# Attention and feed-forward on one core: the range check read from sums that other steps already make

## The chip, the cores and the metric

The kernel runs on one core of a Trainium2 chip. The metric is the device time of the whole launch in microseconds (us), and the lower the better. The core has a matrix engine (PE, whose weight loads the profile lists as PEld), VectorE (DVE), ScalarE (ACT), GpSimd (POOL) and SyncE (SP), which here only starts transfers. Each engine works through its own instructions strictly in order.

## The reference

Attention of four batches, eight heads, 768 tokens, 64 columns a head; a token sees itself and the 95 before it, and the first eight tokens of its batch. Its output, 3072 rows of 512, goes through a feed-forward layer with 2048 hidden columns.

```python
scores = scale * np.matmul(q, k.transpose(0, 1, 3, 2)) + bias          # bias: -slope * distance
scores = np.where(keep, scores, -1000000000.0)
a = np.exp(scores - max); a = a / (sum(a) + 1e-09)
x = np.matmul(a, v)                                                    # then heads side by side: 3072 x 512
h = x @ w_in                                                           # 512 -> 2048
g = np.where(h >= 1, h, np.where(h <= -1, 0.0, (h + 1) ** 2 / 4.0))
out = g @ w_out                                                        # 2048 -> 512
```

All data is f32. The kernel keeps that accuracy with f16 matmuls: a number is split into a high half (its f16 rounding) and a low half (what is left), and three products of halves stand for one product.

## The kernel before, in words

**Tiling.** 24 units of 128 tokens (four batches of six) go through attention. Two units make a chunk of 256 tokens; 12 chunks go through the feed-forward layer, each in eight groups of 256 hidden columns. A unit fetches q, k and v blocks (L754), splits them (high half on ACT, L760; low half on POOL or DVE, L767 to L776), computes scores on PE (L821), adds bias and finds maxima (DVE, L640), takes exponentials with their sums (ACT, L652), splits (L835, L837), turns the result by a transposing transfer on SP's queue (L844), multiplies by v on PE (L862), scales by the reciprocal sums to `x` (DVE, L702), splits that (`xh`: ACT L876, DVE L878), and turns it by another transposing transfer (`xt`, L886).

**Feed-forward.** `ffn1` (L947) makes the 24 matmuls of a group, `h`, in PSUM. `gelu` works on it in steps: s0 on ACT (L970, `u` = relu of h plus a constant, which comes from the one-column tile `half`; the same instruction sums its result into a column of `su`), s1 and s2 on DVE (L980: max; L982: min and product). Steps s3 on split the result into `ga` and `gb`: additions and the low halves on POOL (L992 to L996, L1001, L1006), the high halves on ACT (L999, L1004). From chunk 3 on the second product is made from sums and differences of blocks (L1060, folded into the output `ob` at L1111); the first three chunks use plain products (L1016, with `ob` written at L1133). Hence `u_g` of chunk 10, group g, passes ACT, DVE, POOL, ACT, POOL before PE can use it.

**Weights.** During the first 100 us the weights are split as well: `w_bits` and `wd` on DVE (L535, L539, L543), `woh` and `wd` on ACT (L556, L563), `wol` on POOL (L575).

**The range check.** The fast path holds only for inputs in a certain range. Tests write statistics into columns of the tile `stat`: minima, sums, squares `sq`, the sums `su`. ACT squares each fetched block of q, k and v in place and sums the squares into a column of `sq` (`conv_check`, L784). `verdict` (L1147) compares all of it with limits on DVE, step 0 in ten small instructions (L1150, nine on L1163 and L1164), and where a limit is passed a second, general program runs (`general_path`).

**Order.** Every step is entered in a list `plan` with `at(time, function, ...)`. The written table `PLACE` (L107) then says in which order the plan's steps are issued:

```python
with tc.manual_schedule():
    for n in PLACE or range(len(plan)):
        t, _, f, args = plan[n]
        f(*args)
```

A second written table, `SLOTS`, names the buffer of every tile. Semaphores are placed by the framework from what each instruction reads and writes.

Of the kernel before, what the change touches and what calls it, by code (L numbers as in the profile page):

```python
# [9 lines left out]
F16 = mybir.dt.float16  # L10
F32 = mybir.dt.float32
I32 = mybir.dt.int32
AF = mybir.ActivationFunctionType
# [4 lines left out]
P = 128  # L18
# [14 lines left out]
SV = 256.0  # L33
SW = 4096.0
# [7 lines left out]
NQKV = 3 * NU - B  # L42
W_MAX = NQKV
# [42 lines left out]
CHK = 5.61  # L86
# [203 lines left out]
TPO = 0  # L290
EARLY = 5
R4 = 9
GM = "d"
WL = "pppppppppppppppppppppppppppppppp"
LATE = 8.11
SB = [-25.236754012213545, -6.90594381646442]
# [1206 lines left out]
```

## Time and profile before

| | us |
|---|---|
| runs | 592.34, 591.11, 590.81 |
| median | 591.11 |
| profiled execution, its span | 589.9 |
| PE busy in it | 573.4 (97%) |
| DVE, ACT, POOL busy | 466.4, 442.7, 499.2 |

The profile's span runs from the first to the last instruction. The launch's own time is measured from outside and has some time around the span; for the profiled execution only the span is known, and it is 1.2 us below the median of the runs. A busy share is the part of the span in which an engine had an instruction at work. In a list of instructions the brackets at a row's end say how long the engine stood idle before it and what ended that. The granted clock, PEclk, is 1.00 where TensorE runs at 2.4 GHz and 0.50 where it runs at 1.2 GHz.

### The profile page before, as it was taken

How to read it: one execution, taken by the hardware profiler on the slowest of the kernel's cores; microseconds unless marked ns; L12 is line 12 of the kernel's file. 1: busy time of each engine (PE TensorE's matmuls, PEld its weight loads, DVE VectorE, ACT ScalarE, POOL GpSimd, SP SyncE). 2: the span in 40 equal slices, each digit the busy share in tenths (PEclk: the TensorE clock that was granted, in tenths of full speed). 3: DMA queues.
4: the chain of work that ended last, by engine and by line, in shares of the span. 5: the costliest groups of instructions: out<-in, count | busy, mean ns of one | idle time of the engine just before them, and what ended most of it. 6: DMA issues, size and time to landing. Idle time of an engine off the chain costs nothing.

```text
span 589.9 us, 16477 instructions
## 1 busy us (share of the span) xinstructions
PE 573.4 (97%) x6243; PEld 476.1 (81%) x6243; DVE 466.4 (79%) x1151; ACT 442.7 (75%) x1154; POOL 499.2 (85%) x570
## 2 busy tenths in 40 slices
PE   7999999998999999999999999999999999999995
PEld 5777765456777688987888888889888889898884
DVE  7999999987986767686887977878979877884321
ACT  6999999987956988776986887868868768635340
POOL 0799999977899999899899998799799799579771
PEclk9999999998999999999999999999999999999999
DMA  8796764896650654959856768777688767350011
GB/s 265 235 301 214 236 215 143 184 161 136 131 125 11 144 114 90 192 139 194 211 148 141 133 185 177 179 188 185 153 157 163 184 160 164 87 123 2 1 37 42
DMA packets 145003, 89.24 MB, mean 151 GB/s; under 512 B 108436, under 2 KB 125076, under 8 KB 144916
## 3 DMA queue, kind: packets, MB, share of 16 engines
q1 hardware_dynamic: 144912, 88.10, 60.7%
q8 instruction: 51, 0.84, 0.6%
q14 instruction: 36, 0.29, 0.2%
q10 hardware_dynamic: 4, 0.00, 0.0%
HBM read 54.53 MB, written 6.29 MB: 103 GB/s over the span
## 4 chain that ended last, share of the span: by engine, by line
PE 77%; DVE 9%; ACT 6%; DMA 5%; issue 2%; SPq 0%; DVEq 0%; ACTq 0%
PE h L947 36%; PE o L1060 27%; PE o L1016 5%; PE s L821 4%; PE av L862 4%; DMA pt<-ph 2%; DVE wd L543 2%; ACT z L652 1%; DMA xt<-xh 1%; DVE u L982 1%; DVE w_bits L539 1%; DVE h L980 1%; DMA wd<-in_moe_w_in_dram 1%; DVE w_bits L535 1%; ACT wd L563 1%
## 5 line engine op out<-in xcount | busy, mean ns | idle before, releaser
L947 PE MATMUL h<-xt,wih 128*128 128x256 f16 x1536 | 257.5, 274 | 2.8 <-DMA xt<-xh 2.0
L947 PE MATMUL h<-xt,wil 128*128 128x256 f16 x768 | 210.2, 274 | 0.0
L947 PEld LDWEIGHTS <-wih 128*128 128x128 f16 x1536 | 148.9, 98 | 27.0 <-DVE u L982 3.8
L980 DVE SCALAR_TENSOR_TENSOR h<-h,u 128x512 f32<-128x512 f32 x96 | 66.4, 693 | 37.8 <-ACT u L970 37.5
L1001 POOL TENSOR_TENSOR ga<-u,ga 128x512 f16<-128x512 f32 x72 | 86.9, 1209 | 10.3 <-ACT ga L999 10.1
L652 ACT ACTIVATE z<-z,stat 128x256 f32<-128x256 f32 (+1 forms) x192 | 91.5, 479 | 3.5 <-DVE stat L640 3.1
L1060 PEld LDWEIGHTS <-ga 128*128 128x128 f16 x864 | 83.1, 98 | 10.1
L970 ACT ACTIVATE u<-h,half 128x512 f32<-128x512 f32 x96 | 65.2, 679 | 31.3 <-PE h L947 20.8
L947 PEld LDWEIGHTS <-wil 128*128 128x128 f16 x768 | 75.3, 98 | 9.1
L992 POOL TENSOR_TENSOR u<-u 128x256 f32<-128x256 f32 x72 | 61.5, 856 | 21.0 <-DVE u L982 19.8
L1006 POOL TENSOR_TENSOR gb<-u,gb 128x384 f16<-128x384 f32 x72 | 71.1, 990 | 5.8 <-ACT gb L1004 5.7
L1060 PE MATMUL o<-wd,ga 128*128 128x256 f16 x432 | 70.8, 273 | 0.0
L1060 PE MATMUL o<-woh,ga 128*128 128x256 f16 x288 | 70.7, 273 | 0.0
L999 ACT ACTIVATE ga<-u 128x512 f16<-128x512 f32 x72 | 44.4, 622 | 34.9 <-POOL u L994 26.7
L1060 PEld LDWEIGHTS <-gb 128*128 128x128 f16 x648 | 62.3, 98 | 8.1 <-issue 0.6
L982 DVE SCALAR_TENSOR_TENSOR u<-u,h 128x512 f32<-128x512 f32 x96 | 65.2, 680 | 3.4 <-issue 0.2
L837 DVE SCALAR_TENSOR_TENSOR ph<-z,ph 128x1024 f16<-128x1024 f32 x40 | 54.8, 1373 | 13.3 <-ACT ph L835 13.2
L640 DVE CUSTOM_DVE_ANT_0 z<-s,bias 128x256 f32<-128x256 f32 x160 | 58.9, 414 | 5.8 <-PE s L821 5.7
L1016 PE MATMUL o<-woh,ga 128*128 128x512 f16 x192 | 61.8, 380 | 0.9 <-ACT ob L1133 0.9
L1060 PE MATMUL o<-wd,gb 128*128 128x256 f16 x432 | 60.4, 273 | 0.6 <-DVE ob L1111 0.6
L607 DVE TENSOR_REDUCE stat<-c_raw 128x1 f32<-128x256 f32 x128 | 48.7, 407 | 8.2 <-DMA c_raw<-in_moe_w_in_dram 5.2
L1016 PEld LDWEIGHTS <-ga 128*128 128x128 f16 x288 | 27.2, 98 | 30.2 <-issue 1.9
(131 smaller groups left out, 1166.3 us busy)
## 6 DMA issues: line engine op xcount, KB each, us to landing
wd<-in_moe_w_in_dram SPq DMA_DIRECT2D x16, 512.0 KB, 4.7
wd<-in_moe_w_out_dram SPq DMA_DIRECT2D x16, 512.0 KB, 4.2
c_raw<-in_moe_w_in_dram SPq DMA_DIRECT2D x32, 256.0 KB, 3.2
c_raw<-in_moe_w_out_dram SPq DMA_DIRECT2D x32, 256.0 KB, 3.2
kr<-in_k_dram SPq DMA_DIRECT2D x28, 256.0 KB, 3.8
vr<-in_v_dram SPq DMA_DIRECT2D x28, 256.0 KB, 3.7
qr<-in_q_dram SPq DMA_DIRECT2D x24, 256.0 KB, 4.1
out_dram<-ob SPq DMA_DIRECT2D x23, 256.0 KB, 3.3
```

What stands on the lines that cost most here:

```text
L640: nc.vector.tensor_tensor_reduce(out=p32[u, hf][:, hh, :], in0=pts[u, hf][hh // 2][:, hh % 2, 0:n], in1=(own_bias if n == P else bias)[:, ...
L652: nc.scalar.activation(z, z, AF.Exp, bias=nm[:, c : c + 1], scale=-1.0, accum_out=sums[:, c : c + 1])
L837: nc.vector.scalar_tensor_tensor(phs[u, hf][:, 1, :], zf, SP_, phs[u, hf][:, 0, :], op0=ALU.mult, op1=ALU.subtract)
L947: nc.tensor.matmul(hp[:, :, e, :], w[:, dc, f], xt[:, hf, 2 * a + j, :], start=(n == 0), stop=(n == 3 * NDC - 1),)
L970: nc.scalar.activation(u, h, AF.Relu, bias=half, scale=2.0 / (SV * SW), accum_out=su[:, col : col + 1])
L980: nc.vector.scalar_tensor_tensor(h, h, 4.0 / (SV * SW), u, op0=ALU.mult, op1=ALU.max)
L982: nc.vector.scalar_tensor_tensor(u, u, 4.0, h, op0=ALU.min, op1=ALU.mult)
L992: nc.gpsimd.tensor_sub(f[:, 3:7:3], f[:, 0:6:5], f[:, 4:5].to_broadcast([P, 2, P]))
L1001: nc.gpsimd.tensor_sub(gas[c, g][:, 1], f[:, 0:4], gas[c, g][:, 0])
L1006: nc.gpsimd.tensor_sub(gbs[c, g][:, 1, 0:3], f[:, 4:7], gbs[c, g][:, 0, 0:3])
L1016: nc.tensor.matmul(po, a, w[:, f, :], start=(f == 0 and n == 0), stop=(f == NFC - 1 and n == 2))
L1060: nc.tensor.matmul(acc[:, e], x, w, start=first and n == 0, stop=last and n == 2)
```

## The change

- The 68 instructions of `conv_check` are gone (24 blocks of k, 24 of v, 20 of q), and their 68 columns of `stat`.
- In their place the scaling to `x` (L702 before, L699 after) sums its result into a column of `sq`, for the 40 half units behind the first four units.
- `gelu`'s step s0 takes its constant as a number and sums nothing; the sum `su` is now made by step s2 on DVE.
- A new step `overflow` of four tiny instructions (one on ACT, one on POOL, two on DVE, the last of which writes three columns) tests what the engines make of a conversion that overflows f16.
- `x` is scaled by 128 in place of 256; the limits in `verdict` change.
- `PLACE` is numbered anew for the shorter plan.

```diff
 def scale_x(u, hf):
+    col = 2 * (u - B) + hf
     nc.vector.scalar_tensor_tensor(
-        x, avs[u, hf], SV if u < B else 1.0 / SP_, rs[u, hf].unsqueeze(2).to_broadcast([P, 4, D]),
-        op0=ALU.mult, op1=ALU.mult,
+        x, avs[u, hf], XV if u < B else XV / (SV * SP_), rs[u, hf].unsqueeze(2).to_broadcast([P, 4, D]),
+        op0=ALU.mult, op1=ALU.mult, accum_out=sq[:, col : col + 1] if u >= B else None,
     )
-def conv_check(u, kind, j):
-    b, i = UNITS[u]
-    after(("lo", kind, b, j))
-    r = fetched[u, kind, j]
-    col = {"v": 0, "k": NU, "q": 2 * NU - B}[kind] + (u if kind == "q" else b * NB + j)
-    scale = 1.0 if he(kind, u) != "v" else SV if kind == "v" else SQK
-    nc.scalar.activation(r, r, AF.Square, scale=scale, accum_out=sq[:, col : col + 1])
...
 def gelu(c, g, s):
     if s == 0:
-        col = c * (NFC // 2) + g
-        nc.scalar.activation(
-            u, h, AF.Relu, bias=half, scale=2.0 / (SV * SW), accum_out=su[:, col : col + 1]
-        )
+        nc.scalar.activation(u, h, AF.Relu, bias=2.0, scale=2.0 / (XV * SW))
     elif s == 1:
-        nc.vector.scalar_tensor_tensor(h, h, 4.0 / (SV * SW), u, op0=ALU.mult, op1=ALU.max)
+        nc.vector.scalar_tensor_tensor(h, h, 4.0 / (XV * SW), u, op0=ALU.mult, op1=ALU.max)
     elif s == 2:
-        nc.vector.scalar_tensor_tensor(u, u, 4.0, h, op0=ALU.min, op1=ALU.mult)
+        col = c * (NFC // 2) + g
+        nc.vector.scalar_tensor_tensor(
+            u, u, 4.0, h, op0=ALU.min, op1=ALU.mult, accum_out=su[:, col : col + 1]
+        )
...
+def overflow(s):
+    if s == 0:
+        nc.scalar.activation(c16[:, 0:1], probe[:, 0:1], AF.Copy, scale=SQK)
+    elif s == 1:
+        nc.gpsimd.tensor_add(c16[:, 1:2], probe[:, 0:1], probe[:, 1:2])
+    elif s == 2:
+        nc.vector.scalar_tensor_tensor(
+            c16[:, 2:3], probe[:, 0:1], -SV, probe[:, 1:2], op0=ALU.mult, op1=ALU.subtract
+        )
+    else:
+        nc.vector.tensor_single_scalar(cint, c16.bitcast(I16), 0x7FFF, op=ALU.bitwise_and)
+        nc.vector.tensor_single_scalar(rest[:, 3:6], cint, float(0x7C00), op=ALU.is_equal)
...
 def verdict(s):
-            (sq[:, 0:W_MAX], sq[:, 0:W_MAX], ALU.is_le, 3.6e9),
+            (sq[:, 0:W_MAX], sq[:, 0:W_MAX], ALU.is_le, 1.0e30),
-        nc.vector.tensor_reduce(rest[:, 3:4], stat[:, 0 : marks[4] + 3], axis=AX.X, op=ALU.min)
+        nc.vector.tensor_reduce(rest[:, 6:7], stat[:, 0 : marks[4] + 6], axis=AX.X, op=ALU.min)
-        nc.vector.tensor_single_scalar(su, su, 4000.0, op=ALU.is_le)
+        nc.vector.tensor_single_scalar(su, su, 60000.0, op=ALU.is_le)
```

On PE, SP and POOL the instructions stand in the same order as before, but for one tiny addition on POOL. On ACT the squares are missing. On DVE the three tiny instructions of `overflow` are new, and one block stands elsewhere. Three places of the order follow; a row there gives the line, the operation, what it writes and reads, and the size.

The first is DVE near the end of the attention work. In the kernel before, the block of `verdict` (L1150 to L1164) stands directly ahead of the last unit's two `x` (L702). `h_5`, `h_6` and their `u` belong to groups 5 and 6 of chunk 10.

```order
L1150 TENSOR_REDUCE stat<-stat 128x16
L1163 TENSOR_SCALAR stat<-stat 128x192 x2
L1163 TENSOR_SCALAR stat<-stat 128x68
L1163 TENSOR_SCALAR stat<-stat 128x64
L1163 TENSOR_SCALAR stat<-stat 128x16
L1163 TENSOR_SCALAR stat<-stat 128x64
L1163 TENSOR_SCALAR stat<-nval 128x1 x3
L1164 TENSOR_REDUCE stat<-stat 128x1
L702 SCALAR_TENSOR_TENSOR x_0_9289<-av_0_9250,r_0_9096 128x256
L878 TENSOR_TENSOR xh_0_9292<-x_0_9289,xh_0_9292 128x256
L702 SCALAR_TENSOR_TENSOR x_1_9349<-av_1_9309,r_1_9154 128x256
L980 SCALAR_TENSOR_TENSOR h_5_9214<-h_5_9214,u_5_9335 128x512
```

In the changed kernel DVE's rows just behind the same `x_1` read (L955 and L958 are the gelu's two DVE steps, L867 the low half of `xh`, L1144 to L1158 the block):

```order
L955 SCALAR_TENSOR_TENSOR h_5_9142<-h_5_9142,u_5_9263 128x512
L867 TENSOR_TENSOR xh_1_9281<-x_1_9277,xh_1_9281 128x256
L958 SCALAR_TENSOR_TENSOR u_5_9263,stat<-u_5_9263,h_5_9142 128x2x256
L1144 TENSOR_REDUCE stat<-stat 128x16
L1157 TENSOR_SCALAR stat<-stat 128x192 x2
L1157 TENSOR_SCALAR stat<-stat 128x40
L1157 TENSOR_SCALAR stat<-stat 128x64
L1157 TENSOR_SCALAR stat<-stat 128x16
L1157 TENSOR_SCALAR stat<-stat 128x64
L1157 TENSOR_SCALAR stat<-nval 128x1 x3
L1158 TENSOR_REDUCE stat<-stat 128x1
L955 SCALAR_TENSOR_TENSOR h_6_9104<-h_6_9104,u_6_9296 128x512
```

The whole block has moved behind the last unit's two `x`, whose sums it now reads, and behind the gelu of group 5; it stands directly ahead of the gelu of group 6.

The second place is ACT around 95 to 101 us, where the last weights are split. Before, with `qh_3` the high half of a block of q, `z` exponentials and `woh` weights:

```order
L988 ACTIVATE ga_7_1479<-u_7_1357 128x512
L784 ACTIVATE vr_2_1007,stat<-vr_2_1007 128x512
L760 ACTIVATE qh_3_1492<-qr_3_1354 128x512
L652 ACTIVATE z_0_1484,stat<-z_0_1484,stat 128x256 x4
L652 ACTIVATE z_1_1499,stat<-z_1_1499,stat 128x256
L835 ACTIVATE ph_0_1526<-z_0_1484 128x1024
L556 ACTIVATE woh<-wd 128x512
L563 ACTIVATE wd<-wd 128x512
```

After:

```order
L966 ACTIVATE ga_7_1474<-u_7_1354 128x512
L757 ACTIVATE qh_3_1486<-qr_3_1351 128x512
L648 ACTIVATE z_0_1479,stat<-z_0_1479,stat 128x256 x4
L648 ACTIVATE z_1_1493,stat<-z_1_1493,stat 128x256
L824 ACTIVATE ph_0_1520<-z_0_1479 128x1024
L552 ACTIVATE woh<-wd 128x512
L559 ACTIVATE wd<-wd 128x512
```

The square of a block of v is gone and nothing else has moved; it is the same at the other 67 squares.

The third place is ACT at 123 to 129 us, ahead of the turning of `xh_1`. Before:

```order
L760 ACTIVATE vh_3_1968<-vr_3_1856 128x512
L876 ACTIVATE xh_0_2023<-x_0_1961 128x256
L1048 ACTIVATE wd<-df_1852 128x1024
L784 ACTIVATE qr_5_1615,stat<-qr_5_1615 128x512
L784 ACTIVATE vr_3_1856,stat<-vr_3_1856 128x512
L652 ACTIVATE z_1_2035,stat<-z_1_2035,stat 128x256
L876 ACTIVATE xh_1_2051<-x_1_1956 128x256
```

After:

```order
L757 ACTIVATE vh_3_1959<-vr_3_1848 128x512
L865 ACTIVATE xh_0_2014<-x_0_1952 128x256
L1026 ACTIVATE wd<-df_1844 128x1024
L648 ACTIVATE z_1_2025,stat<-z_1_2025,stat 128x256
L865 ACTIVATE xh_1_2040<-x_1_1947 128x256
```

Two squares that stood ahead of `xh_1` are gone.

## Rows read from the trace of the kernel before

**Rows 1.** The page's list of busy time, share of the span and instructions.

```profile
PE 573.4 (97%) x6243; PEld 476.1 (81%) x6243; DVE 466.4 (79%) x1151; ACT 442.7 (75%) x1154; POOL 499.2 (85%) x570
```

**Rows 2.** Stretches: us, PE, PEld, DVE, ACT, POOL busy, PEclk, DMA share, GB/s.

```profile
80.00:100.00 20.00, 20.00 (x148) 10.74 (x146) 19.83 (x44) 19.96 (x50) 19.54 (x18) 1.00 0.63 197
...
120.00:140.00 20.00, 17.73 (x220) 11.14 (x220) 16.61 (x40) 16.12 (x44) 15.95 (x14) 0.91 0.83 162
...
260.00:280.00 20.00, 18.72 (x207) 16.67 (x206) 13.91 (x27) 14.14 (x35) 18.54 (x23) 1.00 0.79 178
```

**Rows 3.** PE's instructions with waits: start us, us, engine, line, operation, tiles, [idle <-releaser].

```profile
105.18 0.38 PE L1016 MATMUL o<-woh,ga 128*128 128x512 f16 x1 [0.95 <-ACT ob L1133]
...
135.32 0.58 PE L947 MATMUL h<-xt,wih 128*128 128x256 f16 x2 [1.96 <-DMA xt<-xh]
```

**Rows 4.** Chain of waits that ended last: start us, us, what.

```profile
100.52 0.53 ACT woh L556
...
268.20 8.54 DMA pt<-ph
...
534.85 2.62 PE o L1060 x24
```

**Rows 5.** The squares' line on ACT, 82 to 106 us and the whole span.

```profile
82.00:106.00 24.00, 3.54 (x10) 1.00 0.60 169
...
0.00:590.00 590.00, 47.78 (x136) 1.00 0.61 151
```

**Rows 6.** ACT groups: busy us, mean ns of one, idle before.

```profile
L970 ACT ACTIVATE u<-h,half 128x512 f32<-128x512 f32 x96 | 65.2, 679 | 31.3 <-PE h L947 20.8 <-POOL gb L1006 6.6 <-POOL ga L1001 2.5
L970 ACT ACTIVATION_READ_ACCUMULATOR u<-h,half 128x1 f32 x96 | 18.5, 193 | 0.0
L1133 ACT ACTIVATE ob<-o 128x512 f32<-128x512 f32 x6 | 3.4, 581 | 0.0
```

**Rows 7.** DVE's instructions at 95.9 to 100 us.

```profile
95.95 0.08 DVE L640 DVE_READ_ACCUMULATOR2_ANT stat<- 128x1 f32 x1
95.95 0.41 DVE L640 CUSTOM_DVE_ANT_0 z<-s,bias 128x256 f32<-128x256 f32 x1
...
99.46 0.68 DVE L543 SCALAR_TENSOR_TENSOR wd<-wd,w_bits 128x512 int32<-128x512 int32 x1
```

**Rows 8.** DVE and SP's queue at 127 to 133 us.

```profile
128.97 0.58 DVE L878 TENSOR_TENSOR xh<-x,xh 128x256 f16<-128x256 f32 x1 [1.08 <-ACT xh L876]
...
127.35 2.17 SPq L844 DMA_TRANSPOSE pt<-ph  x1
129.62 2.80 SPq L886 DMA_TRANSPOSE xt<-xh  x2
```

**Rows 9.** DVE around the verdict's block, 518 to 530 us.

```profile
518.90 4.34 DVE L1163 TENSOR_SCALAR stat<-stat 128x192 f32<-128x192 f32 x6
523.46 0.78 DVE L1164 TENSOR_REDUCE stat<-stat 128x1 f32<-128x599 f32 x1
...
525.72 0.42 DVE L702 SCALAR_TENSOR_TENSOR x<-av,r 128x256 f32<-128x256 f32 x1 [0.24 <-PE av L862]
...
526.99 0.68 DVE L982 SCALAR_TENSOR_TENSOR u<-u,h 128x512 f32<-128x512 f32 x1
...
528.38 0.69 DVE L982 SCALAR_TENSOR_TENSOR u<-u,h 128x512 f32<-128x512 f32 x1
```

**Rows 10.** The block's six comparisons: ns min/median/max, first and last start.

```profile
L1163 DVE TENSOR_SCALAR stat<-stat x6: 181/996/1174, 518.9 to 523.1; 128x192 f32<-128x192 f32 x2, 128x64 f32<-128x64 f32 x2, 128x68 f32<-128x68 f32 x1, 128x16 f32<-128x16 f32 x1
```

**Rows 11.** POOL's instructions around the same block.

```profile
518.67 2.45 POOL L1001 TENSOR_TENSOR ga<-u,ga 128x512 f16<-128x512 f32 x2
...
527.74 0.72 POOL L992 TENSOR_TENSOR u<-u 128x256 f32<-128x256 f32 x1 [3.73 <-DVE u L982]
...
529.49 0.73 POOL L992 TENSOR_TENSOR u<-u 128x256 f32<-128x256 f32 x1
...
532.25 2.27 POOL L1001 TENSOR_TENSOR ga<-u,ga 128x512 f16<-128x512 f32 x2 [0.20 <-ACT ga L999]
```

More of the change, by code (lines that the diff above doesn't have):

```diff
@@ L12 @@
 I32 = mybir.dt.int32
+I16 = mybir.dt.int16
 AF = mybir.ActivationFunctionType
@@ L33 @@
 SV = 256.0
+XV = 128.0
 SW = 4096.0
@@ L40 @@
 SC = SQK * SQK
-NQKV = 3 * NU - B
-W_MAX = NQKV
+NXS = 2 * (NU - B)
+W_MAX = NXS
 W_MIN = W_MAX + 4 * NFC
@@ L85 @@
 KG = 0.88
-CHK = 5.61
 VCONV = 8.11
@@ L292 @@
 R4 = 9
-GM = "d"
 WL = "pppppppppppppppppppppppppppppppp"
@@ L316, in attention_then_moe @@
     ng, nl = nval[:, 0:1], nval[:, 1:2]
-    half = cpool.tile([P, 1], F32, name="half")
-    nc.gpsimd.memset(half, 0.5 * 4.0)
     one = cpool.tile([P, 1], F32, name="one")
@@ L322, in attention_then_moe @@
     badi = cpool.tile([1, 1], I32, name="badi")
-    sizes = (NU * H, NU * H, NSQ, NFC, 4, NSU)
+    probe = cpool.tile([P, 2], F32, name="probe")
+    nc.gpsimd.memset(probe, 1.0e6)
+    sizes = (NU * H, NU * H, NSQ, NFC, 7, NSU)
     marks = [sum(sizes[:n]) for n in range(len(sizes) + 1)]
@@ L328, in attention_then_moe @@
     with ExitStack() as fast:
-        fast_path(fast, tc, q, k, v, nraw, nval, w_in, w_out, out, half, one, stat, marks, badi)
+        fast_path(fast, tc, q, k, v, nraw, nval, w_in, w_out, out, one, probe, stat, marks, badi)
     bad = nc.values_load(badi, min_val=0, max_val=P)
@@ L342, in to_f32, with fast_path @@
     nc.vector.scalar_tensor_tensor(dst, lo, 29, t, op0=ALU.logical_shift_right, op1=ALU.bitwise_or)
-def fast_path(ctx, tc, q, k, v, nraw, nval, w_in, w_out, out, half, one, stat, marks, badi):
+def fast_path(ctx, tc, q, k, v, nraw, nval, w_in, w_out, out, one, probe, stat, marks, badi):
     nc = tc.nc
@@ L901, in put_unit @@
                 at(t + 2.4, keep_glob, u, "k")
-            at(t + CHK, conv_check, u, kind, j)
         if i >= 2:
@@ L911, in put_unit @@
                 at(t + 2.4, keep_glob, u, "v")
-            at(t + CHK, conv_check, u, "v", j)
         if i >= 2:
@@ L954, in fast_path @@
     gas, gbs = {}, {}
-    def square(c, g):
-        return GM[min(c * (NFC // 2) + g, len(GM) - 1)] == "s"
     def gelu(c, g, s):
-        after(("g", c, g, (None, 0, 10 if square(c, g) else 1, 2, 3, 4, 4, 6, 5, 8, 1)[s])) if s else None
+        after(("g", c, g, (None, 0, 1, 2, 3, 4, 4, 6, 5, 8)[s])) if s else None
         did.add(("g", c, g, s))
@@ L968, in gelu @@
         if s == 0:
+            nc.scalar.activation(u, h, AF.Relu, bias=2.0, scale=2.0 / (XV * SW))
+        elif s == 1:
+            nc.vector.scalar_tensor_tensor(h, h, 4.0 / (XV * SW), u, op0=ALU.mult, op1=ALU.max)
+        elif s == 2:
             col = c * (NFC // 2) + g
-            nc.scalar.activation(
-                u, h, AF.Relu, bias=half, scale=2.0 / (SV * SW), accum_out=su[:, col : col + 1]
-            )
-        elif s == 1 and square(c, g):
-            nc.gpsimd.tensor_scalar(u, u, 4.0, 1.0, op0=ALU.min, op1=ALU.mult)
-        elif s == 10:
-            nc.scalar.activation(u, u, AF.Square)
-        elif s == 2 and square(c, g):
-            nc.vector.scalar_tensor_tensor(u, h, 16.0 / (SV * SW), u, op0=ALU.mult, op1=ALU.max)
-        elif s == 1:
-            nc.vector.scalar_tensor_tensor(h, h, 4.0 / (SV * SW), u, op0=ALU.mult, op1=ALU.max)
-        elif s == 2:
-            nc.vector.scalar_tensor_tensor(u, u, 4.0, h, op0=ALU.min, op1=ALU.mult)
+            nc.vector.scalar_tensor_tensor(
+                u, u, 4.0, h, op0=ALU.min, op1=ALU.mult, accum_out=su[:, col : col + 1]
+            )
         elif c < NP:
@@ L1143, in put_out @@
             nc.sync.dma_start(out[r0 : r0 + P, e * CH : (e + 1) * CH], obs[c, t][:, e])
+    c16 = const.tile([P, 3], F16, name="c16")
+    cint = const.tile([P, 3], I16, name="cint")
+    def overflow(s):
+        if s == 0:
+            nc.scalar.activation(c16[:, 0:1], probe[:, 0:1], AF.Copy, scale=SQK)
+        elif s == 1:
+            nc.gpsimd.tensor_add(c16[:, 1:2], probe[:, 0:1], probe[:, 1:2])
+        elif s == 2:
+            nc.vector.scalar_tensor_tensor(
[4 more added lines that the diff above has]
+            nc.vector.tensor_single_scalar(rest[:, 3:6], cint, float(0x7C00), op=ALU.is_equal)
     vps = {}
@@ L1163, in verdict @@
                 nc.vector.tensor_single_scalar(dst, t, lim, op=op)
-            nc.vector.tensor_reduce(rest[:, 3:4], stat[:, 0 : marks[4] + 3], axis=AX.X, op=ALU.min)
+            nc.vector.tensor_reduce(rest[:, 6:7], stat[:, 0 : marks[4] + 6], axis=AX.X, op=ALU.min)
         elif s == 1:
-            nc.vector.tensor_single_scalar(su, su, 4000.0, op=ALU.is_le)
-            nc.vector.tensor_reduce(peak[:, 0:1], stat[:, marks[4] + 3 :], axis=AX.X, op=ALU.min)
+            nc.vector.tensor_single_scalar(su, su, 60000.0, op=ALU.is_le)
+            nc.vector.tensor_reduce(peak[:, 0:1], stat[:, marks[4] + 6 :], axis=AX.X, op=ALU.min)
             nc.vector.tensor_scalar(peak[:, 0:1], peak[:, 0:1], -1.0, 1.0, op0=ALU.mult, op1=ALU.add)
@@ L1178, in put_ffn1 @@
             at(t + GEL[s], gelu, c, g, s)
-            if s == 1 and square(c, g):
-                at(t + GEL[1] + 0.6, gelu, c, g, 10)
     def put_ffn2(c, ts, g, t):
@@ L1299, in fast_path @@
             at(R1 + DIFF[0] + DIFF[1] * g + 0.9 * x, diff, g, x)
+    for n in range(4):
+        at(CK0 + 4.0 * n, overflow, n)
     for n, d in enumerate((12.0, 9.0, 8.5, 8.0)):
```

310 rows, old and new, of the table PLACE are left out of this document.

## The prediction, as it was put on record before the changed kernel ran

> **What bounds the kernel now.** I read the page's busy times first: the matrix engine works for 573.4 of 589.9 us [rows 1], so all its gaps together are 16.5 us, and no relief of another engine can give back more. The table of stretches shows where the gaps lie: from 80 to 100 us PE, DVE, ACT and POOL are all within half a microsecond of full; from 260 to 280 us ACT works for only 14.14 of 20 us, and PE loses 1.28 us, at a clock of 1.00 [rows 2]. From 120 to 140 us PE loses 2.27 us of work, and the granted clock is 0.91, so another 20 x 0.09 = 1.8 us go to the lower clock. PE's own list names the large waits that ACT could have a part in: 0.95 us for `ob` from ACT at 105.18, and 1.96 us at 135.32 for the turning transfer of `xh` [rows 3]. Last I read the chain of waits: behind 140 us it is PE, group after group, but for a transfer of 8.54 us at 268.20, which is what the 1.28 us were lost to, and at its end the products at 534.85, which run into the last folds [rows 4].
>
> **The 68 squares.** Each is an instruction and a read of its sum: 47.78 us of ACT for 136 instructions, 0.70 us a pair [rows 5]. That is a tenth of ACT's work, and nearly all of it lies beside a PE that has no gap; there it is worth nothing, and the cover is PE itself. Two places are left.
>
> First, the end of the weights' conversion. Five pairs, 3.54 us, stand between 82 and 106 us [rows 5], where ACT is full and the chain ends on `woh` at 100.52 [rows 4] and then on `ob`. But `woh` also needs DVE: L543 starts at 99.46 and takes 0.68 [rows 7], so `woh` can't start before 100.14 plus a signal. ACT becomes free up to 3.5 us earlier and then waits for DVE; the gain is bounded by 0 and by the 0.95 us wait at 105.18 [rows 3]. I take 0.3, what DVE leaves of 100.52 - 100.14.
>
> Second, the wait of 1.96 us at 135.32. Two squares stand ahead of `xh_1` on ACT, and DVE's low half of it waited 1.08 us for ACT [rows 8]. That would free the transfer `xt` by 1 us; but SP's queue holds `pt` from 127.35 to 129.52, back to back with what is ahead, and starts `xt` at 129.62 [rows 8]. I count nothing here; a rival prices it.
>
> **Gelu's step s0.** The relu with a constant from a tile and a sum costs 679 ns and 193 ns for the read [rows 6]; a copy of the same size from PSUM without either costs 581 ns [rows 6]. That is some 0.1 us of busy time and a read for each of the 96, all on ACT beside a full PE: nothing. A group has 2.62 us of PE [rows 4] and passes ACT once, so it comes a little earlier to DVE, which then holds it no longer than before.
>
> **The sums on DVE.** 96 reads behind step s2 and 40 behind `x` are new. Such reads stand behind L640: 0.08 us, but the next instruction starts at the same time, 95.95 [rows 7]. So the pace costs about 0.01 us each. Only the 16 groups of chunks 0 and 1, which meet a full DVE before 100 us, can count: 0.2 us. Bounds: 0 if nothing is held up, 16 x 0.19 = 3.0 us if a read costs what ACT's does [rows 6]; 0.2 is by the row of the same engine. `overflow` adds four instructions on three columns, early and off every chain named here: nothing.
>
> **The verdict's block.** This is where I expect the time to change. Before, the block runs from about 518.8 to 524.24: a tiny reduction, six comparisons in 4.34 us, three small ones and a last reduction [rows 9]. PE doesn't wait for it there. After the change it stands behind step s2 of group 5, which starts at 526.99 and ends at 527.67 [rows 9], and ahead of the gelu of group 6. So steps s1 and s2 of group 6, which end at 529.07 [rows 9], come later by the block's length L. The block's old place ahead of `x` becomes free, but group 5 is not earlier for that: the second `x` ahead of it, at 525.72, waits for PE [rows 9].
>
> Behind s2 of group 6 stands POOL: its first addition at 529.49, then the rest until the two low halves, 532.25 to 534.52 [rows 11]. That is 5.03 us from start to end, and none of it can be passed. PE uses the second of these low halves in the third of the 24 matmuls that start at 534.85, at 534.85 + 2 x 2.62/24 = 535.07 [rows 4]. Group 6 is ready at 529.07 + L, so the low half at 534.1 + L, and with 0.1 us for the signals PE waits L - 0.9 us.
>
> How long is L? The six comparisons cost 181 ns at the least, 996 at the median and 1174 at the most [rows 10], and the form with 16 columns is among them, so their width doesn't set it. POOL was subtracting all the while, 1.2 us an instruction [rows 11], and the long comparisons have about that length. After the change POOL has work from 527.74 to 529.5, then nothing, because it waits for group 6 [rows 11]. Behind the comparisons, which end at 518.90 + 4.34 = 523.24, it lasts to 523.46 + 0.78 = 524.24, 1.0 us more [rows 9]. With nothing of POOL against it the block takes 0.1 + 6 x 0.18 + 1.0 = 2.2 us. If the first three comparisons are held until 529.5, L is 529.5 - 527.67 + 3 x 0.18 + 1.0 = 3.4. As it stands in the row it is 5.4. I take 2.8, the middle of the first two, since POOL's idle time after 529.5 follows from the order: PE waits 1.9 us. PE is the chain from there to the last folds [rows 4], so this is not given back. The ends are 1.3 and 4.5.
>
> The Trainium skill bears on this: "SBUF — State Buffer", section "SBUF: two separate sides", says that VectorE and GpSimd share one pair of ports, which whichever of the two starts first holds for its whole instruction while the other is blocked. The trace agrees in that comparisons of one kind last 181 or 1174 ns [rows 10]. By that rule the block is short where POOL has nothing to do, which is the range 2.2 to 3.4; by the row alone, without a reason for its length, it would be 5.4 and the total about 2.5 us higher.
>
> **The sum.** Span 589.9 - 0.3 (weights' end) + 0.2 (reads on DVE) + 1.9 (block) = 591.7. The runs' median is 1.2 us above the profiled span; with that, 592.9 us.
>
> **Rivals.**
> A. Squares do count at 133 us. `xh_1` comes 1 us earlier, and fetches of q, k, v no longer wait for ACT's squares to free their buffers. If SP's queue is earlier by even 0.7 us, the wait of 1.96 us goes to 1.3. A wait of that size need not lower the clock: the 1.28 us behind the transfer at 268.20 left it at 1.00 [rows 2]. That gives 0.7 + 1.8 = 2.5 us back. With the block's 1.9 the time is 592.9 - 2.5 = 590.4, with its lowest value 589.8. For it: ACT's wait in [rows 8]. Against it: SP's queue in the same rows. It ends at no change or faster.
> B. The block is as long as before, and the wait lowers the clock as at 133 us: 4.5 + 1.8 in place of 1.9 gives 597.3. For it: the median of 996 ns [rows 10], and a wait of 1.96 us that did lower the clock. Against it: POOL has nothing to subtract once it waits. Where only the clock falls and L is 2.8, it is 594.7.
> C. A read of a sum on DVE costs 0.19 us as on ACT. From 16 such reads 3.0 us in the weights' stretch, less half a microsecond of DVE's idle time there: 595.2. Against it: [rows 7].
> D. Fetches start earlier and meet the turning transfers, as the one of 8.54 us [rows 4] shows can happen; one more such collision costs 1.3 us, one fewer gives that back: 594.2 or 591.6. Nothing in the profile says which.
> E. The block's wait isn't there, because PE has something else to wait for or group 6 is not needed so soon: 592.9 - 1.9 = 591.0. The change then does nothing to the time, though the squares are gone. It decides if the block ends before 528.6, which no sum of the rows gives.
> F. The constant doesn't become an immediate but a tile again; then s0 stays near 679 ns, and the time is the same.
>
> **How the numbers follow.** My forecast with its sizes between 1.3 and 2.5 us of wait: 0.40, and its own range is 592.3 to 593.5. A: 0.20. B: 0.19, half of it with the clock alone. C: 0.04. D: 0.08, half each way. E: 0.09. F changes no time. About 0.3%, 1.8 us, is what a measurement of this kernel can tell from no change, so "same" reaches from 589.3 to 592.9. Slower: half of the forecast (0.20), B, C and half of D, 0.47 together. Faster: the part of A in which the block is short or E holds as well, down to 591.0 - 2.5 = 588.5, 0.17. Same: the rest, that is the other half of the forecast, most of E, half of D and a little of A, 0.36. The range of 588.8 to 596.2 holds A and E, the bounds of the block, the clock's fall, and C and D.
>
> **What would show it.** Right: DVE's block directly behind s2 of group 5 near 527.5 us, with POOL idle behind it, and a new wait of PE of 1 to 3 us in the products that started at 534.85, released by POOL's `ga`; the wait at 105.18 shorter by some 0.3 us and the one at 135.32 about as it was; the relu at 580 ns; DVE's reads of 0.08 us with the next instruction at the same start. Wrong: no wait of PE between 530 and 545 (E), a clock of 1.00 from 120 to 140 us (A), DVE's reads with a pace of their own in the first 100 us (C), or PE's busy time in the first 100 us lower by more than 0.5 us.

## The result, and the profile after

The changed kernel is slower: 594.39 us, median of 7 runs (591.98 to 598.33), against 590.81 us for the kernel before, median of 7 (589.47 to 592.34). The ratio is 1.0056, with an interval of 1.0033 to 1.0079. The forecast was 592.9, slower by about 0.3%. Timed twice more, the change gave 1.0039 and 1.0085 (below). The profiled execution has a span of 592.3 us and took 594.39, so 2.1 us lie around the span.

The page's busy times after, to be held against [rows 1]:

```profile
PE 572.1 (97%) x6243; PEld 475.7 (80%) x6243; DVE 469.9 (79%) x1290; ACT 386.4 (65%) x923; POOL 498.5 (84%) x571
```

ACT has lost 56 us of work, and PE still needs its 572. PE's waits of over 0.5 us behind 60 us, in the changed kernel:

```profile
94.80 1.52 PE L810 MATMUL s<-kh,qh 64*128 64x128 f16 x48 [0.64 <-DVE wd L539]
103.97 0.38 PE L994 MATMUL o<-wol,ga 128*128 128x512 f16 x1 [0.60 <-POOL wol L571]
105.95 0.38 PE L994 MATMUL o<-woh,ga 128*128 128x512 f16 x1 [0.74 <-ACT ob L1111]
136.28 0.38 PE L934 MATMUL h<-xt,wih 128*128 128x256 f16 x2 [2.15 <-DMA xt<-xh]
...
276.44 0.87 PE L851 MATMUL av<-vh,pt 128*128 128x64 f16 x24 [1.55 <-DMA pt<-ph]
...
460.93 1.52 PE L810 MATMUL s<-kh,qh 64*128 64x128 f16 x48 [0.62 <-DVE x L699]
...
537.32 0.28 PE L1038 MATMUL o<-wd,ga 128*128 128x256 f16 x1 [1.43 <-POOL ga L979]
578.60 4.09 PE L1038 MATMUL o<-wd,gb 128*128 128x256 f16 x36 [0.60 <-DVE ob L1089]
```

The two waits of [rows 3] are both still there, at 105.95 and 136.28. New are 0.64 us at 94.80, 0.62 at 460.93 and 1.43 at 537.32; the one at 103.97 was 0.42 before, the one at 276.44 was 1.28. PE's order is the same in both kernels, so the start of one and the same instruction can be subtracted. Worked out from the two traces, in us:

| PE's instruction starts | before | after | later by |
|---|---|---|---|
| scores at the end of the weights | 94.00 | 94.80 | 0.79 |
| `av` behind them | 112.72 | 113.69 | 0.97 |
| `h` behind the wait for `xt` | 135.32 | 136.28 | 0.96 |
| scores soon behind it | 139.70 | 138.99 | -0.71 |
| `av` behind a turning transfer | 276.79 | 276.44 | -0.35 |
| scores | 460.42 | 460.93 | 0.51 |
| products of [rows 4] | 534.68 | 535.50 | 0.81 |
| `h` behind them | 537.30 | 539.73 | 2.43 |

So the 2.4 us between the two spans come from five stretches, one of them with the other sign: +0.97 by 113 us (0.08 of it already there at 84 us), -1.67 at 135 to 140, +0.36 from there to 277, +0.86 from there to 460 (0.70 of it at 460 itself), and +1.92 from 530 to 540. The -1.67 belongs to the execution of before, whose granted clock was below 1.00 there [rows 2]; it is 1.00 there in twelve of the fourteen traces kept, four of them of kernels with only a part of the change. Stretches of 12 us around that place, before and then after, with the columns of [rows 2]:

```profile
130.00:142.00 12.00, 9.73 (x135) 7.13 (x134) 9.22 (x23) 8.98 (x24) 9.49 (x8) 0.86 0.80 173
```

```profile
130.00:142.00 12.00, 9.74 (x147) 7.30 (x146) 11.42 (x28) 9.09 (x22) 10.17 (x8) 1.00 0.77 175
```

Equal PE work and the longer wait, but the clock stays at 1.00 after.

The new wait at 537 is the one that was forecast. The chain of waits of the changed kernel runs through the verdict's block into it:

```profile
528.30 1.70 DVE stat L1157 x9
...
530.02 0.75 DVE stat L1158
530.77 0.62 DVE h L955
...
531.48 0.71 DVE u L958 x2
...
532.26 0.72 POOL u L970
...
535.00 0.50 POOL ga L979
...
536.11 1.17 POOL ga L979
...
537.32 2.58 PE o L1038 x22
```

and on DVE the block stands directly behind `u` of group 5 (compare [rows 9]):

```profile
527.51 0.68 DVE L958 SCALAR_TENSOR_TENSOR u<-u,h 128x512 f32<-128x512 f32 x1
...
528.12 0.18 DVE L1144 TENSOR_REDUCE stat<-stat 128x16 f32<-128x32 f32 x1
528.21 1.59 DVE L1157 TENSOR_SCALAR stat<-stat 128x192 f32<-128x192 f32 x6
...
530.02 0.75 DVE L1158 TENSOR_REDUCE stat<-stat 128x1 f32<-128x574 f32 x1
530.69 0.69 DVE L955 SCALAR_TENSOR_TENSOR h<-h,u 128x512 f32<-128x512 f32 x1
```

The block's length is 530.69 - 528.12 = 2.57 us; its six comparisons took 1.59 where they had taken 4.34. POOL was not idle beside them:

```profile
528.28 0.77 POOL L970 TENSOR_TENSOR u<-u 128x256 f32<-128x256 f32 x1 [4.10 <-DVE u L958]
529.12 0.45 POOL L972 TENSOR_TENSOR u<-u 128x128 f32<-128x128 f32 x1
529.65 0.47 POOL L974 TENSOR_TENSOR u<-u 128x128 f32<-128x128 f32 x1
```

```profile
L1157 DVE TENSOR_SCALAR stat<-stat x6: 160/215/781, 528.2 to 529.6; 128x192 f32<-128x192 f32 x2, 128x64 f32<-128x64 f32 x2, 128x40 f32<-128x40 f32 x1, 128x16 f32<-128x16 f32 x1
```

Worked out from the traces, a long comparison ends 0.03 to 0.12 us behind the POOL instruction that it ran beside, in both kernels. POOL's instructions beside the block took 0.9 to 1.3 us before; here they take 0.45 to 0.77, and two of the six comparisons are long (0.78 and 0.45 us).

The wait at 94.80 was not forecast. It goes back to one instruction on DVE, the low half of a block of v. Before, DVE and POOL at 84 to 86 us:

```profile
84.39 0.69 DVE L770 SCALAR_TENSOR_TENSOR vh<-vr,vh 128x512 f16<-128x512 f32 x1
...
84.52 1.58 POOL L575 TENSOR_TENSOR wol<-wd,woh 128x512 f16<-128x512 f32 x1 [0.22 <-ACT wd L563]
```

After:

```profile
84.51 1.65 DVE L767 SCALAR_TENSOR_TENSOR vh<-vr,vh 128x512 f16<-128x512 f32 x1
...
84.46 1.15 POOL L571 TENSOR_TENSOR wol<-wd,woh 128x512 f16<-128x512 f32 x1
```

Before, DVE started 0.13 us ahead and POOL's instruction was the long one; after, POOL started 0.05 us ahead, and DVE's took 0.96 us more. POOL's wait of 0.22 us for ACT is gone as well.

### The profile page after: what moved, and what is told of

The parts are those of the page before. It is cut to its first block, busy times and chain, and to the rows that moved or that the text cites. A ratio compares the mean times of both kernels' runs of the same rounds, so it can differ in the third digit from the quotient of the medians.

```text
span 592.3 us, 16404 instructions
## 1 busy us (share of the span) xinstructions
PE 572.1 (97%) x6243; PEld 475.7 (80%) x6243; DVE 469.9 (79%) x1290; ACT 386.4 (65%) x923; POOL 498.5 (84%) x571
## 4 chain that ended last, share of the span: by engine, by line
PE 72%; DVE 14%; DMA 5%; ACT 4%; issue 3%; POOL 1%; SPq 0%; DVEq 0%; ACTq 0%; POOLq 0%
PE h L934 32%; PE o L1038 25%; PE o L994 5%; PE av L851 4%; PE s L810 4%; DVE wd L539 2%; ACT z L648 2%; DVE w_bits L535 2%; DMA wd<-in_moe_w_in_dram 2%; DVE u L958 2%; DVE z L636 1%; DMA pt<-ph 1%; DVE w_bits L531 1%; DVE h L955 1%; DMA c_raw<-in_moe_w_out_dram 1%
## 5 line engine op out<-in xcount | busy, mean ns | idle before, releaser
L955 DVE SCALAR_TENSOR_TENSOR h<-h,u 128x512 f32<-128x512 f32 x96 | 66.4, 693 | 36.8 <-ACT u L953 36.5
L953 ACT ACTIVATE u<-h 128x512 f32<-128x512 f32 x96 | 56.4, 591 | 54.0 <-PE h L934 32.3
L970 POOL TENSOR_TENSOR u<-u 128x256 f32<-128x256 f32 x72 | 60.3, 841 | 24.1 <-DVE u L958 24.0
L958 DVE SCALAR_TENSOR_TENSOR u<-u,h 128x512 f32<-128x512 f32 x96 | 65.3, 681 | 3.2
L826 DVE SCALAR_TENSOR_TENSOR ph<-z,ph 128x1024 f16<-128x1024 f32 x40 | 56.2, 1407 | 11.2 <-ACT ph L824 11.2
```

The lines of the kernel that those rows point to most:

```text
L826: nc.vector.scalar_tensor_tensor(phs[u, hf][:, 1, :], zf, SP_, phs[u, hf][:, 0, :], op0=ALU.mult, op1=ALU.subtract)
L953: nc.scalar.activation(u, h, AF.Relu, bias=2.0, scale=2.0 / (XV * SW))
L955: nc.vector.scalar_tensor_tensor(h, h, 4.0 / (XV * SW), u, op0=ALU.mult, op1=ALU.max)
L958: nc.vector.scalar_tensor_tensor(u, u, 4.0, h, op0=ALU.min, op1=ALU.mult, accum_out=su[:, col : col + 1])
L970: nc.gpsimd.tensor_sub(f[:, 3:7:3], f[:, 0:6:5], f[:, 4:5].to_broadcast([P, 2, P]))
```

## The experiments

Two theories stood behind them. The block at its new place costs PE 1.9 us; and the sums on DVE lose it the start at 84 us, for 0.6 to 1 us. The rivals: the new waits are scatter of one execution; the sums cost something everywhere; the squares' absence moves POOL and so decides the start at 84 us. Times are medians, with the ratio to before on the same chip and its interval.

**The changed kernel again.** 

> The changed kernel once more, beside the kernel before. Theory: the three new waits of its trace each have a cause in the program: PE's 1.43 us at 537.3 (verdict's block ahead of gelu 6, fixed by the order), 0.64 us at 94.8 (a low half of v on VectorE that took 1.65 us at 84.5 in place of 0.69, because GpSimd had started 0.05 us ahead of it) and 0.62 us at 460.9 (a reduction of weights that waited for its transfer). The first must come again, between 1.1 and 1.8 us. Rival: all three are the scatter of one execution; then the wait at 537 is away or the one at 94.8 comes and goes. Time: 2 to 4 us above before by the theory, within 1 us of it by the rival.

593.57 us against 591.00, ratio 1.0039 (1.0019 to 1.0059). PE's waits: 0.63 at 95.43, and 1.43 at 535.72 once more. The low half of v took 1.66. At 460 only 0.13 us is left, and the wait at 276 is not there. So the first two belong to the kernel, the last two to the execution.

**The block one gelu later.**

```diff
...
+        order.remove(find["verdict", 0])
+        order.insert(order.index(find["gelu", 10, 6, 2]) + 1, find["verdict", 0])
...
```

> The changed kernel with verdict's block one gelu later on VectorE, behind group 6, where VectorE stands idle for 5.75 us. Theory: PE's wait of 1.43 us at 537 goes and nothing takes its place, so the time falls by 1.4 to 1.9 us against the changed kernel and stays 1 to 2 us above before (the rest is ahead of 530 us). Rival: PE's wait there has another cause (an early output of the step before, or the sums), and stays; the time is that of the changed kernel.

PE runs through the products without a wait, where the third matmul had stood for 1.43 us:

```profile
532.57 0.27 PE L934 MATMUL h<-xt,wil 128*128 128x256 f16 x1
532.68 0.49 PE L1038 MATMUL o<-wd,ga 128*128 128x256 f16 x3
```

The block itself became longer, beside POOL instructions of 0.57, 0.74 and 0.95 us, and it cost nothing:

```profile
527.11 2.31 DVE L1157 TENSOR_SCALAR stat<-stat 128x192 f32<-128x192 f32 x6
```

The time is 592.58 us, ratio 1.0029 (1.0003 to 1.0055), 1.0 us under the changed kernel on that chip. The trace confirms the cause; the time moved that way, by less than was expected, and the two intervals overlap.

**Only the block moved, in the kernel before.** The same two lines, with the gelu of group 5 in place of 6.

> The kernel before with only verdict's block moved to where the changed kernel has it, between the gelus of groups 5 and 6 of chunk 10; squares, constant and sums as before. Theory: PE waits 1.4 to 1.9 us for POOL's low half at about 537, and the time is 1.4 to 1.9 us above before. Rival: without the new sums VectorE has slack for the block; the wait is under 0.5 us and the time that of before.

594.20 us, ratio 1.0040 (1.0019 to 1.0061), and the same wait:

```profile
537.10 0.28 PE L1060 MATMUL o<-wd,ga 128*128 128x256 f16 x1 [1.43 <-POOL ga L1001]
```

So the block's move alone makes the kernel slower, by 0.40% or 2.4 us, where PE loses 1.93 us in the trace; neither new sums nor missing squares are needed for it.

**Only the squares out, in the kernel before.**

```diff
+    nc.gpsimd.memset(sq[:, 0:W_MAX], 0.0)
...
-        nc.scalar.activation(r, r, AF.Square, scale=scale, accum_out=sq[:, col : col + 1])
```

This kernel leaves out the squares' part of the range check.

> The kernel before without the 68 squares; their columns of the statistics are set to zero once, so their part of the range check is left out. Nothing else is moved. Theory of the prediction: 0 to 0.4 us faster than before, since PE is full nearly everywhere; ScalarE's busy time falls by 47 us, the wait at 105 us becomes 0.3 us shorter, the one at 135 us stays at 1.5 to 2.2. Rival A of the prediction: the wait at 135 us falls under 1.3 us and the time by 1 to 2.5 us. Second rival: ScalarE's earlier work shifts who comes first at a port, and the weights' stretch becomes longer by up to 1 us.

590.56 us, ratio 0.9988 (0.9963 to 1.0013). PE is 0.30 us earlier at 110 us, 109.50 in place of 109.80; 0.07 of that was there at 84 us, and the rest is the wait for `ob`, 0.73 in place of 0.95. But it doesn't last. Three microseconds on, `av` has a new wait, and starts only 0.10 us earlier than the 112.72 of before:

```profile
112.62 0.86 PE L862 MATMUL av<-vh,pt 128*128 128x64 f16 x24 [0.21 <-DVE stat L641]
```

DVE's low half of `ph`, ahead of it, started earlier and took longer. Before, and then without squares:

```profile
110.09 1.56 DVE L837 SCALAR_TENSOR_TENSOR ph<-z,ph 128x1024 f16<-128x1024 f32 x1 [0.67 <-ACT ph L835]
```

```profile
109.78 1.77 DVE L837 SCALAR_TENSOR_TENSOR ph<-z,ph 128x1024 f16<-128x1024 f32 x1 [0.45 <-ACT ph L835]
```

In all ten traces without squares this instruction takes 1.75 to 1.79 us and the new wait is there, 0.19 to 0.23 us; in the four with squares it takes 1.55 to 1.57 and the wait is not there. The wait at 135 did not shrink, and the rows show why:

```profile
127.69 0.41 DVE L878 TENSOR_TENSOR xh<-x,xh 128x256 f16<-128x256 f32 x1
...
127.04 2.13 SPq L844 DMA_TRANSPOSE pt<-ph  x1
129.26 2.87 SPq L886 DMA_TRANSPOSE xt<-xh  x2
...
135.30 0.27 PE L947 MATMUL h<-xt,wih 128*128 128x256 f16 x1 [2.26 <-DMA xt<-xh]
```

`xh` is 1.28 us earlier than in [rows 8], without a wait for ACT; SP's queue takes it up only 0.36 us earlier, behind `pt`. Rival A falls. The low half of v started first and took 0.67, so the missing squares alone don't lose it the start.

**Gelu's sums of two chunks back on ACT.**

```diff
...
+            nc.scalar.activation(
+                u, h, AF.Relu, bias=2.0, scale=2.0 / (XV * SW), accum_out=su[:, col : col + 1] if c < 2 else None
+            )
...
-                u, u, 4.0, h, op0=ALU.min, op1=ALU.mult, accum_out=su[:, col : col + 1]
+                u, u, 4.0, h, op0=ALU.min, op1=ALU.mult, accum_out=su[:, col : col + 1] if c >= 2 else None
```

> The changed kernel, with gelu's sums of the first two chunks made by ScalarE again (as before); all else as changed. In three profiles of kernels with the new sums the low half of v on VectorE at 84.4 took 1.65 us, started 0.05 us behind GpSimd's instruction; in three without them it took 0.7 and started ahead of it. Theory: the reads on VectorE (0.1 us by then) lose it the start; with them on ScalarE it starts first again, takes 0.7, PE's wait of 0.6 us at 94 to 95 goes, and PE is 0.6 to 0.9 us earlier at 113 us. The wait of 1.43 us at 537 stays. Time 0.5 to 1 us under the changed kernel. Rival: GpSimd is the one that moved (ScalarE without squares lets it start earlier); then the instruction still takes 1.65 and the time is that of the changed kernel.

```profile
85.96 0.68 DVE L767 SCALAR_TENSOR_TENSOR vh<-vr,vh 128x512 f16<-128x512 f32 x1
...
85.98 1.68 POOL L571 TENSOR_TENSOR wol<-wd,woh 128x512 f16<-128x512 f32 x1
```

DVE starts 0.02 us ahead and takes 0.68; PE has no wait at 94 to 97, and the one of 1.43 stays, at 537.12. 592.24 us, ratio 1.0013 (0.9992 to 1.0034). This execution was late by 1.7 us already at 18 us, from which comes the shift of both starts. The lead of DVE over POOL at this place, in the traces so far: 0.13 us before, 0.14 with only the block moved, 0.03 without squares, 0.02 here, -0.05 in the changed kernel (twice) and in the one with the block later. So the rival is half right: ACT's relief lets POOL start earlier and takes 0.1 of the lead, but only with the reads on DVE is the start lost.

**Both corrections.** The edits of the last experiment and of the block one gelu later together.

> The changed kernel with both: gelu's sums of the first two chunks on ScalarE, and verdict's block one gelu later on VectorE. Theory: neither the wait at 95 nor the one at 537 is there, and what is left of the change are the missing squares: 0 to 0.6 us faster than before, 2 to 3 us faster than the changed kernel. Rival: the sums of x and of the other chunks cost something of their own; then the time stays 0.5 us or more above before.

589.94 us, ratio 0.9977 (0.9960 to 0.9995). Neither wait is there; the largest that are left lie at 103 (0.55), 105 (0.73), 135.8 (2.22) and 574 (0.59). Timed again beside the changed kernel:

> The kernel of both corrections again, beside the changed kernel on one chip. Theory: no wait at 95 and none at 537; 2 to 4 us below the changed kernel, and 0.5 to 2 us below before. Rival: the 0.9977 of its first timing was luck of that chip; then it is within 0.5 us of before.

591.03 us, ratio 0.9996 (0.9980 to 1.0012); the changed kernel, on the same chip, follows below with 595.60. So both corrections give back the whole loss. That they are faster than before, one timing says and the other doesn't.

**No new sums at all.**

```diff
+    nc.gpsimd.memset(sq[:, 0:W_MAX], 0.0)
+    nc.gpsimd.memset(su, 0.0)
...
-            op0=ALU.mult, op1=ALU.mult, accum_out=sq[:, col : col + 1] if u >= B else None,
+            op0=ALU.mult, op1=ALU.mult,
...
-                u, u, 4.0, h, op0=ALU.min, op1=ALU.mult, accum_out=su[:, col : col + 1]
+                u, u, 4.0, h, op0=ALU.min, op1=ALU.mult
```

This kernel leaves out the part of the range check that reads these sums.

> The changed kernel without any of the new sums on VectorE (neither of x nor of gelu; their columns are set to zero once, so that part of the range check is left out), verdict's block at its new place. Theory: 136 reads fewer are worth what their start at 84 us costs and no more: PE is 0.6 to 0.9 us earlier at 113 us as without the first sixteen, nothing further changes behind it, and the wait of 1.43 us at 537 stays. Rival: reads cost 0.08 us or more each where VectorE is late (around 460 us and in the last chunks); then PE gains at other places as well and the time falls by over 1.5 us against the changed kernel.

The low half of v took 0.67 and PE has no wait at 95; the wait of 1.43 is there, at 538.03, with 0.46 us for ACT's `ga` just ahead of it. The time is 594.34 us (one run of 602.42 among the eight), ratio 1.0037 (1.0024 to 1.0051). The waits at 460 and at the last folds are as long as in the changed kernel, and the one at 276 comes and goes, so sums elsewhere cost nothing that the trace shows. By its trace the time should lie some 0.7 us under the changed kernel; its ratio doesn't show that against the 1.0039 to 1.0085 of other sets of runs. This execution, too, was late by 1.7 us at 18 us.

**Only gelu's edit, in the kernel before.** The edit of the change to s0 and s2, and the verdict's last three steps behind the last gelu (the `order` lines are shown with the last edit below).

> The kernel before with only gelu's edit: constant as a number, sums on VectorE (for that the last steps of the verdict, which read the sums, stand behind the last gelu, as in the changed kernel); the squares and the first block of the verdict are where they were. Theory: reads make VectorE 0.1 us later at 84.4, but GpSimd there waits for ScalarE, which still has its squares, and starts at 84.5; so it is close which starts first. If VectorE does, the time is that of before within 0.3 us; if not, PE is 0.6 to 0.9 us later at 113 us. Rival: the relu's 0.1 us shorter on ScalarE is worth something, and PE is earlier by over 0.3 us at 113 us.

```profile
84.70 1.65 DVE L770 SCALAR_TENSOR_TENSOR vh<-vr,vh 128x512 f16<-128x512 f32 x1
...
84.64 1.16 POOL L575 TENSOR_TENSOR wol<-wd,woh 128x512 f16<-128x512 f32 x1
...
94.96 1.52 PE L821 MATMUL s<-kh,qh 64*128 64x128 f16 x48 [0.63 <-DVE wd L543]
```

With the squares still there, gelu's edit alone loses the start by 0.06 us. PE is 1.15 us late at 110 us (0.26 of it already at 84 us), and yet the time is 590.47 us, ratio 0.9979 (0.9963 to 0.9995). Timed again:

> The kernel before with only gelu's edit and the verdict's last steps behind the last gelu, again. By its trace PE is 1.1 us late at 110 us, for VectorE's instruction on v took 1.65 us again, and yet its times were 0.2% below before. Theory: the times scatter by some us from transfers that meet (0 to 1.6 us at 276, 0 to 0.7 at 460) and from the clock after the wait at 135, and this was a lucky set; it comes out within 0.2% of before or above. Rival: the edit does save something that one trace doesn't show, and it is 0.2% below before again.

590.91 us, ratio 0.9998 (0.9975 to 1.0021), with 1.64 us for the low half of v and 0.64 at 96.36. The second timing is within what the trace says (0.9 us lost behind 84 us, less 0.2 to 0.3 us from the next experiment); the first is not, and I have no cause for it.

**The verdict's last steps right behind the last gelu,** beside both corrections.

```diff
...
+        for st in (3, 2, 1):
+            order.remove(find["verdict", st])
+            order.insert(order.index(find["gelu", 11, 7, 2]) + 1, find["verdict", st])
...
```

> The kernel of both corrections (gelu's sums of two chunks on ScalarE, verdict's block one gelu later) with the verdict's last three steps right behind the last gelu, so that VectorE's last folds no longer stand behind the cast that waits for PE's tiny matmul. Theory: PE's wait of 0.59 us at 574 becomes 0.28 as in the run with gelu's edit alone, the time falls by 0.3 us against the kernel of both corrections and is 1 to 2 us below before. Rival: the wait is the fold's own and stays; no difference.

PE's wait before the last folds, with both corrections and then with this as well:

```profile
572.64 4.09 PE L1041 MATMUL o<-wd,gb 128*128 128x256 f16 x36 [0.60 <-DVE ob L1092]
```

```profile
575.26 4.09 PE L1041 MATMUL o<-wd,gb 128*128 128x256 f16 x36 [0.28 <-DVE ob L1092]
```

0.3 us, as expected. 589.81 us, ratio 0.9976 (0.9957 to 0.9996), 5.8 us below the changed kernel on the same chip. It is the lowest median here, but timed once, and 1.2 us below both corrections on that chip where the trace gives 0.3: the rest is scatter. Whether it is faster than before stays open, as for both corrections.

**The changed kernel a third time.** 

> The changed kernel beside the three others. Theory: the waits of 1.43 us at 537 and of 0.6 us at 95 in its trace; 2 to 3.5 us above before, 2 to 4 us above the kernel of both corrections.

595.60 us, ratio 1.0085 (1.0056 to 1.0115), and in its trace 0.64 us at 94.91, 1.64 for the low half of v, and 1.43 at 536.63. It is 4.6 us above both corrections on one chip.

**All fourteen traces together,** worked out as in the table. From 84 to 113 us PE loses 0.86 to 0.91 us in the six with gelu's sums on DVE in the first two chunks, where the low half of v is the long one; in the eight without, the difference is -0.10 to 0.18. From 530 to 545 us PE loses 1.92 to 1.93 us in five of the six with the block directly ahead of the gelu of group 6 (2.24 without new sums), and 0.00 in the eight others.

## Why the prediction was right, and where its sizes were off

- **The block, +1.9: right.** 2.57 us long where 2.8 was taken; PE's wait is 1.43, and PE is 1.92 us later: 0.3 just ahead of the wait and 1.6 at it, since an idle time is counted from the end of a matmul, 0.27 us behind its start, and the next would have started 0.11 us behind that start. It came in every trace of a kernel with the block there (six of six, 1.43 each) and in none without. That the block's length hangs on POOL was right too; but the comparisons were not short because POOL was idle, as the lower bound of 2.2 took it. POOL worked beside them, in shorter instructions than before.
- **The squares, -0.3: right at its place, nothing in the end.** The wait for `ob` is 0.22 us shorter, and the new wait of 0.21 at `av` takes it back. The text counted the gain as kept without a look at what stands behind it. Rival A failed where the text put the objection against it, at SP's queue.
- **The sums on DVE, +0.2: the mechanism's pace right, the size wrong.** This is the mis-sized term: it measured 0.9. A read takes 82 ns and the next instruction starts with it, and DVE's `u` of 81.39 us starts at 81.50, 0.1 late as worked out, though PE itself is 0.08 late by then:

```profile
L958 DVE DVE_READ_ACCUMULATOR u<-u,h 128x1 f32 x96 | 7.9, 82 | 0.0
```

  That lateness, with ACT's relief, let POOL start ahead of DVE at 84.5, for 0.96 us on DVE, 0.7 on PE at 94 us and 0.9 by 113. That the reads decide the start is shown, by six traces of six with them and none of eight without; how the 0.18 us of lost lead divide between them and ACT's relief is not, for recorded starts are no better than some 0.07 us (below). The prediction had the lock of the ports in hand, from [rows 10 and 11], and used it for the block alone; 0.13 us of lead in a full stretch were there to be read. Behind 113 us the reads cost nothing that a trace shows.
- **The relu, 0: right.** It fell from 679 [rows 6] to 591 ns, beside a full PE:

```profile
L953 ACT ACTIVATE u<-h 128x512 f32<-128x512 f32 x96 | 56.4, 591 | 54.0 <-PE h L934 32.3 <-POOL gb L984 9.6 <-POOL ga L979 6.2
```

  The constant makes the difference, not the sum: with the number as constant, the sixteen that sum again on ACT take no longer (the row is of the run with gelu's sums of two chunks back on ACT).

```profile
L954 ACT ACTIVATE u<-h 128x512 f32<-128x512 f32 x16 | 9.4, 586 | 1.7 <-PE h L934 1.5
```

- **From span to time, +1.2: wrong.** After, 2.1 us lie around the span, and in the runs on record 1.7 to 2.5. The 1.2 set the span of one execution of before against the median time of others. That execution had accidents, 1.67 us of low clock and 1.28 us at 276, but its 589.9 is close to the median spans of the later runs of before, 589.0 to 589.8.
- **The sum.** The terms that belong to the kernel are 0.9 + 1.9 = 2.8 us, where 1.8 were forecast; the times say 2.3 to 5.0. The three wrong sizes (squares, sums, span) all point the same way, so the measured 594.39 lies above 592.9 and above the forecast's own 592.3 to 593.5. With the measured sizes the same sum would give 589.9 + 2.8 + 2.0 = 594.7, an estimate.
- **The signs.** Rival B's fall of the clock did not come: the granted clock is 1.00 from 520 to 580 us. Two of the signs of being wrong did. The clock is 1.00 from 120 to 140 us, A's sign; but the wait there is 2.15 us and not shorter, so it isn't A. And PE's busy time in the first 100 us is 93.67 in place of 94.72 us; the wait of 0.64 us at 94.80 is a part of that.
- **What stays open** is the size of the start at 84 us in the times. Pairs of kernels with and without it, with the block at the same place, differ by nothing (1.0039 for the changed kernel, 1.0037 without new sums, 1.0040 with only the block moved) or by up to 0.5% (1.0029 with the block later, 0.9977 with both corrections), and gelu's edit alone shows no loss. Nor is there a cause for the 5.0 us of the third timing of the change.

## What to carry to other kernels

When an order written by hand is renumbered because a step now reads something later, the moved block's length counts for whatever stood behind its new place: look for a stretch in which its engine is idle, here one gelu later. In a stretch where two engines that hold each other up are both full, ask at each long instruction which of them starts first and by how much; here 0.18 us between them turned it round. A gain at one wait is not kept until the next wait has been looked at: the 0.2 us at `ob` were gone 8 us later. And 48 us taken off an engine that is hardly waited for gave nothing here.

## What the runs showed of the hardware

The low half of v at 84 us (f16 from f32 and f16) took 0.67 to 0.69 us on DVE in the eight traces where DVE got ahead of POOL's `wol`, which then took 1.6 to 1.8, and 1.64 to 1.66 in the six traces where it did not, with 1.15 for `wol`; the pair together needs the same time either way, 1.7 us in the traces of before and after, and only who is late changes. The Trainium skill, "SBUF — State Buffer", section "SBUF: two separate sides", says that the first to start holds the ports for its whole instruction, and the traces agree for this pair, but for one (without new sums) in which DVE's recorded start was 0.07 us behind POOL's and it was short all the same; recorded starts are not that exact. The Trainium skill counts there, beside a GpSimd instruction that reads SBUF, the VectorE ones with two SBUF inputs among those that need the shared ports; the int32 instructions of the weights on DVE have two (0.68 us at 86.08) and kept their length beside POOL, so for these the measurement decides.

The clock fell behind the wait at 135 us in two of the fourteen traces, of 1.96 us in before and of 2.15 with two chunks' sums back on ACT (0.86 from 130 to 142 us in both); it stayed at 1.00 behind 1.92 to 2.30 us in the twelve others, 2.15 in the changed kernel among them. So the length of the wait doesn't tell whether the clock falls behind it. Transfers meet or don't: the wait at 276 was 1.28 and 1.55 us in the traces of before and after and is absent in nine of fourteen. And in four traces the first f32 matmuls at 9 us ran slower, which made PE 0.6 to 1.75 us late at 18 us; a row of one of them, and then the same matmuls in the changed kernel's trace:

```profile
8.87 1.01 PE L624 MATMUL s<-kr,qr 64*128 64x128 f32 x6 [0.16 <-DVE stat L636]
```

```profile
8.87 0.71 PE L624 MATMUL s<-kr,qr 64*128 64x128 f32 x8 [0.37 <-DVE stat L636]
```

Six take 1.01 us there and eight 0.71 here. These accidents of single executions are as large as the terms of this change, so a trace's span can't stand for a kernel's median; differences between two traces can, place by place.
